# Sums of W_out on GpSimd instead of from memory, and a new place for one strip's input loads

## The chip, the cores and the metric

The kernel runs on one core of one Trainium2 chip. The core has a matrix engine (TensorE, PE in the profile), a vector engine (VectorE, DVE), an activation engine (ScalarE, ACT), a general engine (GpSimd, POOL) and a queue processor (SyncE, SP) that issues transfers between the chip's memory (HBM) and the on-chip buffer (SBUF). Matrix products land in a small accumulator memory (PSUM). The metric is the device time of one execution in microseconds, as the median of several runs.

## What is computed

An attention block without softmax, and then a feed-forward block, all in 32-bit floats (the weights of the second block arrive as 64-bit floats and are converted on the chip):

```
kv  = einsum('bhsd,bhse->bhde', k, v)          # 8 batches, 8 heads, 576 tokens, 64 features
att = einsum('bhsd,bhde->bhse', q, kv)
att = att / sqrt(mean(att**2, -1) + 1e-6) * g_norm
x   = att as (8*576, 8*64)                      # 4608 tokens x 512
h   = x @ w_in                                  # 512 -> 2048
out = maximum(h, 0)**2 @ w_out                  # 2048 -> 512
```

## The kernel before

**Strips.** The 4608 tokens are worked on in nine strips of 512 tokens, numbered 0 to 8. Each strip has an "up" stage (x times W_in, with the squared relu) and a "down" stage (the result times W_out). Products of 2 by 2 blocks are made with seven block products instead of eight (the Strassen-Winograd scheme): some blocks are first added or subtracted, and the seven products are then added up. Strip 0 multiplies plainly going up and uses the scheme once going down. Strip 1 uses it once going up and twice, nested, going down. Strips 2 to 8 use it nested both ways, so that each of their stages consists of 7 times 7 small products, and each small product is 16 matrix instructions in the trace (lines 841 to 842).

**The weights of the down stage.** For each of the seven outer products p, W_out has a combined block (`w_out`, in HBM). The inner seven products need, beside three of its quarters (b11, b12, b22, products 1, 2 and 3 in the order of the loop), four further sums, numbered 5, 6, 7 and 4: b12 - b11, then b22 minus that, then b22 - b12, then b21 minus the second. `deep_sums` (line 1028) makes these four on VectorE, once, while strip 0 goes down; `store_deep_sums` (line 969) stores them in `w_deep` in HBM. In every strip from 1 on, `stream` (line 933) loads for each p two tiles of six buffers: three quarters of `w_out` (768 KB) and the four sums of `w_deep` (1024 KB). A buffer is loaded again when TensorE has read what it held.

**The order of the work.** It is written out by hand: the order in which the program emits instructions is the order on each engine. A strip from 2 on has 55 "slots" of the up stage (`up_slot`, line 1248) and then 14 steps of the down stage (`down_deep`, line 1109, two steps for each of the outer products in the order 4, 1, 2, 6, 5, 7, 3). Products 1, 2 and 4 of the first outer product (p = 4) already stand in slots 49, 51 and 53; its products 7, 5, 6 and 3 come in the second step of the down stage:

```
        if k == 0 and s >= DEEP_UP:
            if i == 0:
                return
            for j in (7, 5, 6, 3):
                small_products(s, p, (j,))
```

For the other p, the first step makes products 1, 2, 3, the second 4, 5, 6, 7. VectorE makes the sums on the activations' side (`leaf_steps`, tiles `g_s`, lines 1046 and 289), and adds up the products (`together`, tiles `o_sb`, line 1088). GpSimd works in the up stage: sums of x for the next products (`leaf_x`, `sum_x`, line 289, tiles `x_l` and `x_t`), additions to intermediate results (line 1300, tiles `snap` and `gt`), and at the end of the up stage four additions of activations that the nested down stage needs (`add_s1`, line 1184, `gt<-gt`), one earlier and three in slots 47 to 50. In the down stage it has nothing to do until the last outer product, where it begins the sums of x for the next strip.

**The loads.** All of them are issued on SyncE's queue, in the order of the program; a load waits there for its buffer, and what stands behind it waits too. Loads of keys and values (256 KB each), of the remaining rows of a batch, and of queries (64 KB pieces, in order, called drips) are not emitted where they are used. The main loop (from line 1338, the choice of loads from line 1405) runs a clock of its own, estimated in microseconds per slot, and emits a load when it is due, except where `quiet` holds it back, and not closer together than `least`.

Of the kernel before, what the change touches and what calls it, by code (L numbers as in the profile page):

```python
# [20 lines left out]
def kernel(  # L21
# [198 lines left out]

    w_out = dram.tile([7, P, 2, FQ, P], FP32, name="w_out")

    w_deep = dram.tile([7, P, 4, FQ // 2, P], FP32, name="w_deep")

    w_in_deep = dram.tile([7, P, 3, 2, WN // 2], FP32, name="w_in_deep")

# [706 lines left out]
    def stream(n=1):  # L933
        for _, u in zip(range(n), to_stream):
            p = u[2] if u[0] == "in" else u[1]
            t = stream_pool.tile([P, 4, FQ // 2, P], FP32, name="w_blk", tag="w_blk")
            if u[0] == "in":
                w_blk[u] = t.rearrange("p n f e -> p n (f e)")
                nc.sync.dma_start(out=w_blk[u][:, 0:3], in_=w_in_deep[A_IN[p]].rearrange("p n g e -> p n (g e)"))
            elif len(u) == 2:  # L940
                w_blk[u] = t.rearrange("p (h a) f e -> p h (a f) e", h=2)
                nc.sync.dma_start(out=w_blk[u], in_=w_out[B_OUT[p]])
            elif u[2] == 0:

                nc.sync.dma_start(
                    out=t[:, 1:4], in_=w_out[B_OUT[p]].rearrange("p h (a f) e -> p (h a) f e", a=2)[:, 1:4]
                )
                for i, j in enumerate((3, 1, 2)):
                    w_blk[*u[:2], j] = t[:, i + 1]
            else:  # L950
                nc.sync.dma_start(out=t, in_=w_deep[B_OUT[p]])
                for i, j in enumerate((5, 6, 7, 4)):
                    w_blk[*u[:2], j] = t[:, i]

    def out_tile():
# [13 lines left out]
    def store_deep_sums(p, w):  # L969
        if p in (6, 4):  # L970

            parts = [sum_pool.tile([P, FQ // 2, P], FP32, name=f"w_t{i}", tag="sum") for i in range(4)]
            for _ in deep_sums(parts, w):
                if p == 4:
                    yield
            for i, t in enumerate(parts):
                nc.sync.dma_start(out=w_deep[B_OUT[p], :, i], in_=t)
            return
        if p not in deep:
            reserve(p)  # L980
        t = deep.pop(p)
        deque(deep_sums([t[:, i] for i in range(4)], w), 0)
        nc.sync.dma_start(out=w_deep[B_OUT[p]], in_=t)

    def down(s, p, i):
        if i == 0:
# [71 lines left out]
    LAST_PLACE = {1: (0, 0), 2: (1, 0), 6: (1, 1), 5: (2, 0), 7: (2, 1), 4: (3, 0), 3: (4, 0)}  # L1058
    place = lambda s, p: LAST_PLACE if s == N_STRIP - 1 and p in (5, 3) else PLACE

    def small_products(s, p, js):
        c = "B" if p in (4, 2, 5, 3) else "A"
        if js[0] == 1 and p not in (6, 7, 3):
            opened[c] = set()
            n = 2 + (s == N_STRIP - 1 and p == 5)
            chain[c] = [fpsum.tile([P, 4, P], FP32, name=f"ps_{c}", tag="f") for _ in range(n)]
            if n == 3:
                chain[c].append(apsum.tile([P, 2, 4, P], FP32, name="ps_x", tag="x", bufs=1)[:, 0])
                chain[c].append(apsum.tile([P, 4, P], FP32, name="ps_at", tag="at"))
        for j in js:  # L1070
            x, i = place(s, p)[j]
            a, w = leaf[p][j], w_blk.pop((s, p, j))
            for f in range(FQ // 2):
                halved_product(
                    chain[c][x][:, i, :], a[:, f, :], w[:, f, :], x not in opened[c] and f == 0, f == FQ // 2 - 1
                )
            opened[c].add(x)
# [31 lines left out]
    def down_deep(s, k, i):  # L1109
        p = DEEP_ORDER[k]  # L1110
        if k == i == 0:
            stream()
        if s == N_STRIP - 1 and k == 6 and i == 1:

            o = out_tile()
            q, rest = (t.rearrange("p t (h e) -> p (t h) e", h=2) for t in (o, part[6]))
            at = {j: chain["B"][x][:, i : i + 1] for j, (x, i) in place(s, p).items()}
            sums = {
                1: [(slice(0, 4), 1)], 6: [(slice(1, 2), 2), (slice(2, 4), 6), (slice(0, 1), 6)],
                7: [(slice(2, 3), 5), (slice(2, 3), 7), (slice(0, 1), 5), (slice(3, 4), 7)],  # L1120
                4: [(slice(3, 4), 4)], 3: [(slice(0, 1), 3)],
            }
            for js in ((1,), (2, 6), (5, 7), (4,), (3,)):
                small_products(s, p, js)
                for to, j in sums[js[-1]]:
                    n = to.stop - to.start
                    nc.vector.tensor_tensor(
                        out=q[:, to], in0=rest if j == 1 else q[:, to], in1=at[j].to_broadcast([P, n, P]), op=ALU.add
                    )
                    if (j, to.start) in ((2, 1), (7, 2), (4, 3), (3, 0)):  # L1130
                        eng = nc.scalar if j == 3 else nc.sync
                        send_quarter(s, 0, 1, o, *divmod(to.start, 2), eng)
# [6 lines that stand above are left out]
            stream(2)  # L1139
            deque(leaf_next[1], 0)  # L1140
            for slot in sorted(relus):
                relu_squares(slot)
            for slot in sorted(first_s):
                add_s1(s, slot)
            return
        if k == 6 and i == 1:
            small_products(s, p, (4,))
            return
        if s < N_STRIP - 1 or k < 6:
            small_products(s, p, ((1, 2, 3), (4, 5, 6, 7))[i])  # L1150
        if k < 6:
            stream()
        q11, q12, q21, q22 = (gq[s, q] for q in (11, 12, 21, 22))
        if i == 1:
            if k == 0:
                nc.vector.tensor_tensor(out=q12, in0=q12, in1=q22, op=ALU.add)
            if k == 3:
                minus(nc.vector, q22, q22, q11)
            if k == 4:
                minus(nc.vector, q21, q21, q11)  # L1160
            if k == 6:
                deque(together(s, p), 0)
            return
        if k == 2:
            minus(nc.vector, q11, q12, q11)
        if k == 3:
            leaf_sums(s, DEEP_ORDER[k + 1])
        if k:
            deque(together(s, DEEP_ORDER[k - 1]), 0)
        if k < 6 and k != 3:  # L1170
            leaf_sums(s, DEEP_ORDER[k + 1])
        if k == 6 and s + 1 < N_STRIP:
            leaf_x(s + 1, 0)
            sum_x(s + 1, 5)
            sum_x(s + 1, 6)
            leaf_x(s + 1, 1)
# [71 lines left out]
    def up_slot(s, slot):  # L1248

        for n, p in enumerate(UP_SETS):  # L1250
            i, odd = divmod(slot - 7 * n, 2)
            if not odd and 0 <= i < 7:
                up_small(s, n, p, ORDER[i], slot)
        if slot in SUM_AT:
            sum_x(s, SUM_AT[slot])
        n, at = divmod(slot, 7)
        if at == 0 and 0 < n < 6:
            leaf_x(s, n + 1)
        if s == DEEP_UP and at == 0 and n < 7:
            deep_differences_in(A_IN[UP_SETS[n]])  # L1260
        relu_squares(slot)
        add_s1(s, slot)
        if slot in (1, 3, 5):
            small_products(s - 1, 3, ((slot + 9) // 2,))
        if slot == 5:
            stream()
            deque(together(s - 1, 3), 0)
        if slot == 40:
            leaf_next.update({4: leaf_steps(s, 4), 1: leaf_steps(s, 1)})
        if slot in (49, 51, 53):  # L1270
            small_products(s, 4, ({49: 1, 51: 2, 53: 4}[slot],))
        if slot in (41, 43, 45, 47):
            next(leaf_next[4])
        if slot in (49, 51):
            next(leaf_next[1])
# [62 lines left out]
    for s in range(N_STRIP):  # L1338
# [25 lines left out]
        for i, (w, fn, a) in enumerate(steps):  # L1364
# [33 lines left out]
            if s:  # L1398
                clock[0] += 3.2 if i >= n_up else 2.2 if s == DEEP else 1.2
                soon = tiles_due and tiles_due[0][2][0] // NT == s + 1  # L1400
                if i == n_up + 10:
                    while tiles_due and tiles_due[0][2][0] // NT == s + 1:
                        _, f, a = tiles_due.popleft()
                        f(*a)
                elif not due(keys_due) and not (soon and due(tiles_due)):
                    least = 2.1 if s == DEEP else 4.5 if i < n_up else 3.3
                    quiet = n_up * 2 // 3 < i < n_up + 3 or s == DEEP and i > n_up + 9
                    quiet = quiet or s == DEEP and i < n_up and drips and drips[0][0] == load_q_rest
                    if not quiet and clock[0] >= dripped[0] + least:
                        dripped[0] = clock[0]  # L1410
                        drip(True)
# [73 lines left out]
```

## Time and profile before

| | us |
|---|---|
| median of three runs | 879.48 |
| the three runs | 876.89, 879.48, 882.86 |
| the profiled execution | 876.18 |
| its span in the profile | 874.4 |
| TensorE busy | 860.8 |
| VectorE busy | 722.9 |
| ScalarE busy | 352.0 |
| GpSimd busy | 315.4 |
| median from issue to landing, `w_deep` tile of 1024 KB | 7.2 |
| the same, `w_out` tile of 768 KB | 6.7 |

The span is the time from the first to the last recorded instruction; the execution takes 1.8 us more. TensorE's matrix instructions are pipelined and overlap in the record, so "busy" does not mean that it is at its peak, but an idle stretch of TensorE is a real gap. A digit in the lines of tenths stands for a fortieth of the span (21.9 us), and 9 is 90% or more. The 56 loads of `w_deep` and the 56 of `w_out` are eight strips times seven outer products.

### The profile page before, as it was taken

The numbers are of one execution on the slowest core, as the hardware profiler recorded it, in microseconds if no ns is written. First come the engines' busy times: TensorE is split into PE (matmuls) and PEld (weight loads), VectorE is DVE, ScalarE is ACT, GpSimd is POOL, SyncE is SP. The second block draws the span as 40 slices with busy tenths as digits, with TensorE's granted clock in tenths as the row PEclk, the third lists the DMA queues.
The fourth block names the chain that finished last, engine by engine and source line by source line (L and its number), as shares of the span: only waits on it lengthen the run. The fifth ranks groups of instructions, "written<-read, shape, count | busy, mean of one in ns | idle before, by whom it ended". The sixth has DMA issues, their size and how long they took to land.

```text
span 874.4 us, 32665 instructions
## 1 busy us (share of the span) xinstructions
PE 860.8 (98%) x14176; PEld 805.8 (92%) x14176; DVE 722.9 (83%) x1236; ACT 352.0 (40%) x805; POOL 315.4 (36%) x319
## 2 busy tenths in 40 slices
PE   8999999999999899999999999999999999999998
PEld 7445888889999899999999999999999999999998
DVE  3899998879867896889778977897889777975897
ACT  5799241320047402560358034811392147202710
POOL 1100004630458305650475045704471447144700
PEclk9999999999999999999999999999999999999999
DMA  9998998999988997989778978998668856885483
GB/s 306 328 311 251 285 372 237 283 339 346 305 219 205 338 328 242 239 290 338 245 213 261 344 268 228 271 346 287 189 238 293 295 173 218 299 283 196 175 313 120
DMA packets 170304, 236.49 MB, mean 270 GB/s; under 512 B 79536, under 2 KB 134576, under 8 KB 161840
## 3 DMA queue, kind: packets, MB, share of 16 engines
q1 hardware_dynamic: 169856, 234.33, 82.5%
q8 instruction: 111, 1.82, 0.8%
q14 instruction: 33, 0.27, 0.1%
q10 hardware_dynamic: 304, 0.07, 0.0%
HBM read 197.66 MB, written 36.70 MB: 268 GB/s over the span
## 4 chain that ended last, share of the span: by engine, by line
PE 82%; DVE 9%; DMA 4%; ACT 3%; issue 2%; SPq 1%; DVEq 0%; ACTq 0%
PE ps_A L842 35%; PE ps_B L842 30%; PE ps_C L842 5%; PE ps_A L847 4%; PE x_ps L468 2%; PE kv_ps L432 2%; PE ps_B L847 2%; DVE w_c L269 1%; DVE w_t L289 1%; DMA q<-in_q_dram 1%; DMA w_blk<-w_deep 1%; DMA w_deep<-w_t 1%; DVE wt L289 1%; DMA q_rest<-in_q_dram 1%; PE ps_C L847 1%
## 5 line engine op out<-in xcount | busy, mean ns | idle before, releaser
L842 PE MATMUL ps_B<-w_blk,g_s 128*64 128x128 f32 x2016 | 122.6, 273 | 0.0
L842 PEld LDWEIGHTS ps_B<-w_blk,g_s 128*64 128x64 f32 x2016 | 113.1, 137 | 0.1
L842 PE MATMUL ps_A<-x_l,w_in 128*64 128x128 f32 x1568 | 102.4, 273 | 0.6 <-ACT snap L1305 0.6
L289 POOL TENSOR_TENSOR x_l<-xT 128x256 f32<-128x256 f32 x21 | 15.9, 757 | 232.4 <-PE ps_A L842 184.3
L842 PE MATMUL ps_B<-w_blk,gt 128*64 128x128 f32 x1504 | 94.7, 273 | 2.8 <-DMA w_blk<-w_deep 1.6
L842 PE MATMUL ps_A<-w_blk,g_s 128*64 128x128 f32 x1536 | 92.7, 273 | 0.4 <-issue 0.4
L842 PEld LDWEIGHTS ps_A<-x_l,w_in 128*64 128x64 f32 x1568 | 88.9, 137 | 0.9 <-ACT snap L1305 0.8
L842 PEld LDWEIGHTS ps_B<-w_blk,gt 128*64 128x64 f32 x1504 | 85.1, 137 | 3.6 <-issue 2.2
L1300 POOL TENSOR_TENSOR snap<-snap,gt 128x512 f32<-128x512 f32 x35 | 46.2, 1319 | 113.1 <-ACT snap L1305 107.5
L842 PEld LDWEIGHTS ps_A<-w_blk,g_s 128*64 128x64 f32 x1536 | 86.1, 137 | 0.5 <-issue 0.5
L1305 ACT COPY snap<-ps_A 128x512 f32<-128x512 f32 x63 | 36.8, 585 | 105.0 <-PE ps_A L842 99.0
L1240 ACT ACTIVATE gt<-gt 128x512 f32<-128x512 f32 x112 | 70.1, 626 | 14.2 <-DVE gt L1300 14.2
L1241 ACT ACTIVATE gt<-gt 128x512 f32<-128x512 f32 x112 | 70.7, 631 | 3.6
L842 PE MATMUL ps_A<-w_blk,gt 128*64 128x128 f32 x1152 | 71.5, 273 | 0.0
L842 PEld LDWEIGHTS ps_A<-w_blk,gt 128*64 128x64 f32 x1152 | 65.0, 137 | 0.0
L1089 ACT COPY o_sb<-ps_A 128x128 f32<-128x128 f32 x24 | 6.4, 265 | 145.5 <-PE ps_A L842 110.2
L1088 DVE TENSOR_TENSOR o_sb<-o_sb,ps_B 128x256 f32<-128x256 f32 (+1 forms) x123 | 47.4, 386 | 15.8 <-ACT o_sb L1089 11.0
L289 DVE TENSOR_TENSOR gt<-gt 128x2048 f32<-128x2048 f32 (+1 forms) x29 | 59.7, 2063 | 0.0
L1300 POOL TENSOR_TENSOR gt<-gt,snap 128x512 f32<-128x512 f32 x42 | 52.6, 1282 | 17.7 <-DVE snap L1300 17.7
L842 PE MATMUL ps_B<-x_l,w_blk 128*64 128x128 f32 x784 | 51.3, 273 | 0.0
L842 PE MATMUL ps_A<-x_l,w_blk 128*64 128x128 f32 x784 | 51.2, 273 | 0.0
L1046 DVE TENSOR_TENSOR g_s<-gt 128x512 f32<-128x512 f32 x56 | 47.9, 856 | 0.0
(194 smaller groups left out, 1801.6 us busy)
## 6 DMA issues: line engine op xcount, KB each, us to landing
w_blk<-w_deep SPq DMA_DIRECT2D x56, 1024.0 KB, 7.2
w_blk<-w_out SPq DMA_DIRECT2D x56, 768.0 KB, 6.7
w_blk<-w_in_deep SPq DMA_DIRECT2D x49, 768.0 KB, 6.1
raw<-in_moe_w_in_dram SPq DMA_DIRECT2D x16, 512.0 KB, 7.0
raw<-in_moe_w_out_dram SPq DMA_DIRECT2D x16, 512.0 KB, 4.8
k<-in_k_dram SPq DMA_DIRECT2D x29, 256.0 KB, 4.8
v<-in_v_dram SPq DMA_DIRECT2D x29, 256.0 KB, 5.1
x_d<-x_q SPq DMA_DIRECT2D x27, 256.0 KB, 5.3
```

The costliest lines, as they stand in the source:

```text
L269: yield nc.vector.scalar_tensor_tensor(out=ci, in0=high, scalar=-(2**30), in1=ci, op0=ALU.bitwise_and, op1=ALU.bitwise_or)
L289: eng.tensor_tensor(out=out, in0=a, in1=b, op=ALU.subtract)
L432: nc.tensor.matmul(ps[ts(h, D), i], lhsT=a, rhs=w, start=i == 0 and c == 0, stop=c == C, skip_group_check=True)
L468: nc.tensor.matmul(ps[half, r, i, ts(p, D)], lhsT=q[row, half], rhs=kvd[b, p][row, row], start=True, stop=True)
L842: nc.tensor.matmul(ps[half], lhsT=lhsT[:, half], rhs=rhs, start=start, stop=stop, skip_group_check=True)
L847: nc.tensor.matmul(bank[BANK[p]][:, i, :], lhsT=lhsT(k), rhs=rhs(k), start=p in (1, 5, 2) and i == 0 and k == 0, stop=k == n - 1, skip_gro ...
L1046: nc.vector.tensor_tensor(out=t, in0=a21, in1=a22, op=ALU.add)
L1088: add = lambda out, a, b: nc.vector.tensor_tensor(out=out, in0=a, in1=b, op=ALU.add)
L1240: nc.scalar.activation(o, o, AF.Relu)
L1241: nc.scalar.activation(o, o, AF.Square)
L1300: add = lambda eng, out, a, b: eng.tensor_tensor(out=out, in0=a, in1=b, op=ALU.add)
L1305: nc.scalar.copy(t, ps)
```

## The change

Two things are changed.

The second of the four further sums (number 6) is no longer stored in `w_deep` nor loaded. It is still made on VectorE in strip 0, because the fourth is made from it, but `w_deep` has three parts, and a load of it moves 768 KB into the last three quarters of its buffer. The free first quarter is filled by a new function `second_sum`, which subtracts on GpSimd: quarter b22 of the `w_out` tile minus the first sum. It is emitted for the next outer product in the second step of each but the last, so that it stands one outer product ahead of its use; for p = 4 it is emitted in slot 50 of the up stage (in strip 1, at the first step of the down stage).

The second thing concerns the main loop in strip 2 (`DEEP_UP`). In its slots 25 to 38 keys, values and remaining rows are not emitted when due, and from slot 24 on no queries are; in the first 15 slots of strip 3 queries may follow each other every 2.1 instead of 4.5 us of the loop's clock. In the order of SyncE's queue, two pairs of keys and values, and one pair of remaining rows, move from ahead of strip 2's first two W_out tiles to behind them, and four pairs of query pieces move from strip 2 to the beginning of strip 3. The order on TensorE, VectorE and ScalarE is the same as before; GpSimd's has the 56 new subtractions, seven in a row in each strip from 1 on, with nothing between them.

```diff
-    w_deep = dram.tile([7, P, 4, FQ // 2, P], FP32, name="w_deep")
+    w_deep = dram.tile([7, P, 3, FQ // 2, P], FP32, name="w_deep")
...
-                nc.sync.dma_start(out=t, in_=w_deep[B_OUT[p]])
-                for i, j in enumerate((5, 6, 7, 4)):
+                nc.sync.dma_start(out=t[:, 1:4], in_=w_deep[B_OUT[p]])
+                for i, j in enumerate((6, 5, 7, 4)):
                     w_blk[*u[:2], j] = t[:, i]
...
-            for i, t in enumerate(parts):
+            for i, t in enumerate((parts[0], *parts[2:])):
                 nc.sync.dma_start(out=w_deep[B_OUT[p], :, i], in_=t)
...
-        deque(deep_sums([t[:, i] for i in range(4)], w), 0)
-        nc.sync.dma_start(out=w_deep[B_OUT[p]], in_=t)
+        deque(deep_sums([t[:, i] for i in (1, 0, 2, 3)], w), 0)
+        nc.sync.dma_start(out=w_deep[B_OUT[p]], in_=t[:, 1:4])
...
+    def second_sum(s, p):
+
+        if s >= DEEP:
+            minus(nc.gpsimd, w_blk[s, p, 6], w_blk[s, p, 3], w_blk[s, p, 5])
...
         if k == i == 0:
             stream()
+            if s == DEEP:
+                second_sum(s, p)
+        if i == 1 and k < 6:
+            second_sum(s, DEEP_ORDER[k + 1])
...
+        if slot == 50:
+            second_sum(s, 4)
...
-                elif not due(keys_due) and not (soon and due(tiles_due)):
-                    least = 2.1 if s == DEEP else 4.5 if i < n_up else 3.3
-                    quiet = n_up * 2 // 3 < i < n_up + 3 or s == DEEP and i > n_up + 9
+                elif not (not (s == DEEP_UP and 24 < i < 39) and due(keys_due)) and not (soon and due(tiles_due)):
+                    least = 2.1 if s == DEEP or s == DEEP_UP + 1 and i < 15 else 4.5 if i < n_up else 3.3
+                    quiet = n_up * 2 // 3 < i < n_up + 3 or s == DEEP and i > n_up + 9 or s == DEEP_UP and i > 23
```

## The prediction

> **What bounds the kernel now.** I first read the page: the span, the engines' totals and GpSimd's tenths.
>
> ```profile
> span 874.4 us, 32665 instructions
> PE 860.8 (98%) x14176; PEld 805.8 (92%) x14176; DVE 722.9 (83%) x1236; ACT 352.0 (40%) x805; POOL 315.4 (36%) x319
> ...
> POOL 1100004630458305650475045704471447144700
> ```
>
> TensorE sets the time. All its idle time is 874.4 - 860.8 = 13.6 us, and 4.4 us of that lies in the first 120 us and 2.6 in the last 46, which the change does not touch. So there is little to gain, and any new gap of TensorE is paid in full. GpSimd has one slice at 0 or 1 in nearly every strip, in the down stage. Next, what TensorE waits for, in the list of waits:
>
> ```profile
> PE ps_B L842 <- DMA w_blk<-w_deep: 1.6, 1, 1.6
> ...
> PE ps_B L842 <- DMA w_blk<-w_out: 1.2, 1, 1.2
> ```
>
> In eight strips TensorE waits only twice for a W_out tile. The timeline of TensorE shows both at strip 2's first outer product (slots 49 to 53):
>
> ```profile
> 288.29 1.09 PE L842 MATMUL ps_B<-w_blk,gt 128*64 128x128 f32 x16 [1.17 <-DMA w_blk<-w_out]
> ...
> 290.93 1.07 PE L842 MATMUL ps_B<-x_t,w_blk 128*64 128x128 f32 x16
> 293.64 1.09 PE L842 MATMUL ps_B<-w_blk,gt 128*64 128x128 f32 x16 [1.64 <-DMA w_blk<-w_deep]
> 294.54 1.07 PE L842 MATMUL ps_A<-x_l,w_in 128*64 128x128 f32 x16
> ```
>
> Then I looked at the same place in an undisturbed strip, on GpSimd, TensorE and VectorE (strip 3; the three views in this order):
>
> ```profile
> 380.50 1.67 POOL L1300 TENSOR_TENSOR snap<-snap,gt 128x512 f32<-128x512 f32 x1 [3.62 <-ACT snap L1305]
> 382.13 5.11 POOL L1184 TENSOR_TENSOR gt<-gt 128x512 f32<-128x512 f32 x3
> ```
> ```profile
> 386.29 3.66 PE L842 MATMUL ps_B<-w_blk,g_s 128*64 128x128 f32 x64
> ```
> ```profile
> 384.93 1.17 DVE L289 TENSOR_TENSOR g_s<-g_s,gt 128x512 f32<-128x512 f32 x1
> 386.02 0.68 DVE L1300 TENSOR_TENSOR gt<-ps_B,snap 128x512 f32<-128x512 f32 x1
> ...
> 387.22 0.68 DVE L289 TENSOR_TENSOR g_s<-gt,g_s 128x512 f32<-128x512 f32 x1
> 387.82 0.68 DVE L289 TENSOR_TENSOR g_s<-gt 128x512 f32<-128x512 f32 x1
> ```
>
> The 64 matrix instructions from 386.29 are p = 4's products 7, 5, 6 and 3. GpSimd is still in its three additions until 387.24. Where these overlap a VectorE operation that reads two SBUF tiles (`g_s`), that one takes 1.17 instead of 0.68 us and an addition about 1.72 instead of 1.28; a VectorE operation that reads PSUM stays at 0.68.
>
> **Loads: 256 KB less, 56 times.** 14.7 of 236.5 MB go. From rows of the page, a 768 KB tile lands after 6.7 us and a 1024 KB tile after 7.2, so each lands some 0.5 us sooner. Apart from the two waits above, none of these tiles is late, so this is worth **0**. The stores in strip 0 shrink too; there TensorE's only related gap is 0.3 us, which I leave as a bound.
>
> **Strip 2's loads moved: a gain.** Ahead of the `w_deep` tile issued at 284.87 (it took 8.63 us to land) SyncE's queue held 1 MB of keys and values, 0.25 MB of remaining rows and six query pieces. Its buffer had been read by about 278.4. With those behind it, it should land before 287, and the `w_out` tile, whose buffer was free from 272.3, well before that. Both waits, 1.17 + 1.64 = 2.81 us, go. What is late next is VectorE: the product of 290.93 reads a bank that VectorE finishes at 290.42, in a stretch in which it is busy without a gap (287 to 293.8). Moved up by 1.17 it would start at 289.76, so it waits about 0.6 us. Gain: **2.2 us**, between 0.4 (the second wait stays, and the first is worth 1.17 less VectorE's 0.6, rounded down) and 2.8. The moved keys are used at 336 and have over 40 us to spare. The moved query pieces are different: two sets that VectorE transposes at 353.1 and 354.3 are now issued in strip 3's first slots, partly behind stores that left at 343.6, so the last should land near 351 or 352 by the 3 to 6 us of the rows there. I take 0 for it, with 3 us (half a load's latency) as the far end.
>
> **56 subtractions on GpSimd.** Each is 128x512 with both inputs in SBUF: 1.28 us undisturbed, 1.72 beside VectorE, so 72 to 96 us in all, on an engine with 30 us idle in each down stage. For 49 of them that hides everything: the subtraction of p runs when its `w_deep` tile has landed, on most strips 2.4 to 6 us before product 4 of p reads that tile, and product 6 comes two products (1.75 us) later still. In strip 1 the first tile lands at 196.4 and product 6 starts near 200.7. The seventh subtraction of a strip delays the sums of x for the next strip, which stand behind it in GpSimd's queue: in strip 3 from 417.12 to about 420.4 (the last `w_deep` tile lands at 418.68), in strip 1 from 229.8 to 236. TensorE reads these sums 7.6 to 10.8 us after they are ready, so that costs 0 too.
>
> The other seven are those of p = 4 in strips 2 to 8. They stand in GpSimd's queue behind the three additions, and TensorE needs them at the third of the 64-instruction block's four products, 2 x 0.873 = 1.75 us after its start. After the additions the subtraction takes 1.70 more (beside the two `g_s` of 387.22 and 387.82, at the spacing of the additions before it), and TensorE starts 0.13 later (293.64 after a landing at 293.51).
>
> | strip | additions end | sum ready, TensorE starts (+1.83) | product 6 now | new gap |
> |---|---|---|---|---|
> | 3 | 387.24 | 389.07 | 388.04 | 1.03 |
> | 4 | 476.06 | 477.89 | 477.26 | 0.63 |
> | 5 | 569.76 | 571.59 | 570.36 | 1.23 |
> | 6 | 658.44 | 660.27 | 659.58 | 0.69 |
> | 7 | 746.40 | 748.23 | 747.19 | 1.04 |
> | 8 | 831.97 | 833.80 | 832.77 | 1.03 |
>
> That is **5.65 us**. In strip 2 the additions end at 292.63, so TensorE could start at 294.46, and product 6 (now 297.16) moves to 294.9: no gap. If VectorE does not disturb it, 0.47 less each: 2.8. If each is held up by both `g_s`, 0.45 more: 8.4. Behind the waiting product TensorE's whole queue waits, and later stages have no slack that gives it back.
>
> [...]
>
> **Contention in the down stages.** In the window from 392 to 424 us VectorE is busy 29.8 of 32 us, so it has 0.42 us to spare per outer product (6.11 us). A subtraction takes about 0.47 from it, at worst 1.1 (the longest disturbed `g_s` took 1.8). The sum that TensorE waits for first is ready 2.5 to 4.3 us ahead, so lagging by 0.05 per product costs 0; by 0.7, with seven of them, the lead is gone.
>
> **Sum.** On the profiled execution: 876.2 - 2.2 + 5.65 = 879.6. The median of the runs shown lies 3.3 above that execution, and the result will be a median as well, so 879.5 + 3.45 = **882.9**, rounded to 883.
>
> **Rivals.**
> - *The sum is in time* (the additions finish sooner, or TensorE's queue of weights hides it): only strip 2's gain is left, 879.5 - 2.2 = 877.3, faster than before. For it: 1.72 is needed each time, and an undisturbed subtraction leaves gaps of 0.2 to 0.8 only. Against: in all six strips the additions end 0.8 to 1.2 us before the product. Chance 0.18.
> - *VectorE becomes the bound in the down stages*: decided by 0.42 us to spare against what a subtraction really takes. At 1.1 each, 7 x 0.7 = 4.9 of lag less 2.5 of lead, 2.4 us a strip, eight strips: 19, and with the forecast's 3.45 some 902; at half that, 892. Together with late queries in strip 3: chance 0.12.
> - *The waits in strip 2 don't go* (the tile is held by its buffer or by the stores before it): 879.5 + 5.65 - 0.4 = 884.7. Chance 0.08.
> - The forecast: 0.62.
>
> **Range and chances.** About 1% (8.8 us) is what a measurement of this kernel can tell from no change. From the first rival's 877 to the forecast with the far ends of the sum and the queries, 879.5 - 2.2 + 8.4 + 3 = 888.7, taken at 888. Faster by over 1% would need most of TensorE's 13.6 us: 0.02. Slower by over 1% is the second rival: 0.12. The rest is 0.86.
>
> **What would show it.** Right: TensorE's waits name GpSimd's subtraction (`w_blk`, line 289) six or seven times, near 1 us each, always at the block of 64; the two waits for W_out tiles are gone; `g_s` operations in the down stages are longer on average than now (0.69), and no TensorE wait names them. Wrong: no such wait, waits for `g_s` or `o_sb` in the down stages, or a wait of VectorE's transposes for `q` near 351. The largest risk is a subtraction whose waits for four transfers cost GpSimd more than I can see here.

## The result, and the profile after

The changed kernel takes 881.8 us (median of 22 executions, 876.3 to 887.4) beside 877.2 us for the kernel before (22 executions, 873.5 to 882.9): a ratio of **1.0039 (1.0022 to 1.0057)**, or +3.4 us (1.9 to 5.0); the two medians differ by 4.6 us, which lies inside this interval. The prediction said +3.45, and 882.9 as the time. The total is right, but it came about in another way than was worked out, as the traces show. In the table of the experiments below, one execution of the kernel that holds strip 3's queries and keys too (1122 us at a mean clock of 0.75) is left out.

The page of the changed kernel: span, engine totals, and the tenths of GpSimd.

```profile
span 880.0 us, 32793 instructions
PE 862.8 (98%) x14176; PEld 806.2 (92%) x14176; DVE 755.9 (86%) x1236; ACT 352.5 (40%) x805; POOL 402.6 (46%) x375
...
POOL 1100004622468544743577255735474547455731
```

GpSimd has 56 instructions and 87 us more, and its empty slices in the down stages have filled. VectorE has the same 1236 instructions and 33 us more, which is 0.59 us for each subtraction; without the subtractions it falls back to 723.3 us (an experiment below). TensorE's busy time is 2.0 us longer with the same 14176 instructions, a first sign that some of them ran slower.

What TensorE waits for, in the list of waits (us in total, times, longest):

```profile
PE ps_B L842 <- DMA w_blk<-w_deep: 4.0, 1, 4.0
...
PE ps_B L842 <- DVE g_s L289: 1.7, 1, 1.7
...
PE ps_B L842 <- POOL w_blk L289: 1.2, 3, 0.5
PE ps_B L842 <- DVE snap L1311: 1.1, 1, 1.1
```

Strip 2's two waits are gone, and VectorE's wait of 1.1 us stands in their place. But there are three new ones. The timeline of TensorE shows the largest, in **strip 3**, and the queue of SyncE when the tile was issued (the kernel before, then the changed one):

```profile
381.05 1.04 PE L842 MATMUL ps_B<-w_blk,gt 128*64 128x128 f32 x16
...
378.04 0.38 SPq L951 DMA_DIRECT2D w_blk<-w_deep  x1
```
```profile
378.08 1.04 PE L842 MATMUL ps_B<-w_blk,gt 128*64 128x128 f32 x16
...
380.70 1.04 PE L842 MATMUL ps_B<-x_t,w_blk 128*64 128x128 f32 x16
385.77 1.09 PE L842 MATMUL ps_B<-w_blk,gt 128*64 128x128 f32 x16 [4.03 <-DMA w_blk<-w_deep]
386.67 1.57 PE L842 MATMUL ps_A<-x_l,w_in 128*64 128x128 f32 x16
387.96 4.94 PE L842 MATMUL ps_B<-w_blk,g_s 128*64 128x128 f32 x64
...
381.25 0.38 SPq L951 DMA_DIRECT2D w_blk<-w_deep  x1
```

This is the first `w_deep` tile of strip 3. TensorE came to the first outer product there 2.97 us earlier than before (378.08 and 381.05), but the tile was issued 3.21 us later (381.25, before 378.04) and landed at 385.64. The wait costs more than 4.03 us. The 16 instructions of 386.67 took 1.29 us to the next start, where others take 0.88, and the block of 64 took 4.74 where it takes 3.49. In the table by windows of 2 us (busy time of PE, PEld, DVE, ACT, POOL, then the granted clock, the DMA share and GB/s) the reason is in the column after POOL:

```profile
384.00:386.00 2.00, 0.23 (x4) 0.26 (x6) 0.00 (x0) 1.03 (x2) 0.50 (x2) 1.00 1.00 384
386.00:388.00 2.00, 2.00 (x33) 2.00 (x31) 0.00 (x0) 0.00 (x0) 1.03 (x1) 0.78 0.99 381
388.00:390.00 2.00, 2.00 (x23) 2.00 (x21) 1.73 (x3) 0.97 (x2) 0.05 (x1) 0.50 1.01 418
390.00:392.00 2.00, 2.00 (x36) 2.00 (x34) 0.17 (x1) 0.29 (x1) 1.30 (x1) 0.87 0.38 153
392.00:394.00 2.00, 2.00 (x41) 2.00 (x39) 1.41 (x4) 0.27 (x1) 0.00 (x0) 1.00 0.42 83
```

After the stall the granted clock fell to 0.50. The record of the clock in the trace has it there from 387.10 to 390.51, which agrees with the means of these windows. That is another 0.41 + 1.25 = 1.7 us, and the stall is worth 5.7 in all.

In **strips 4 to 8** TensorE does wait for GpSimd's sum of p = 4, as forecast, but less. Strip 5, on GpSimd, VectorE and TensorE:

```profile
567.79 5.11 POOL L1193 TENSOR_TENSOR gt<-gt 128x512 f32<-128x512 f32 x3
572.87 1.27 POOL L289 TENSOR_TENSOR w_blk<-w_blk 128x512 f32<-128x512 f32 x1
```
```profile
572.88 1.80 DVE L289 TENSOR_TENSOR g_s<-gt,g_s 128x512 f32<-128x512 f32 x1
574.61 1.76 DVE L289 TENSOR_TENSOR g_s<-gt 128x512 f32<-128x512 f32 x1
```
```profile
571.77 1.92 PE L842 MATMUL ps_B<-w_blk,g_s 128*64 128x128 f32 x32
574.19 1.97 PE L842 MATMUL ps_B<-w_blk,g_s 128*64 128x128 f32 x32 [0.51 <-POOL w_blk L289]
```

The subtraction starts as soon as the additions end and takes 1.27 us, as undisturbed ones in this profile do (1.28 at 407.17); it is VectorE's `g_s`, issued 0.01 us later, that takes 1.80 instead of 0.68. By starts of TensorE's instructions the five gaps cost 0.19, 0.72, 0.18, 0.56 and 0.55: 2.2 us.

In **strip 1** TensorE waits for VectorE, whose two `g_s` take 1.69 and 1.10 us instead of 0.68 beside GpSimd's work (GpSimd, VectorE, TensorE):

```profile
233.09 1.28 POOL L289 TENSOR_TENSOR w_blk<-w_blk 128x512 f32<-128x512 f32 x1 [5.49 <-DMA w_blk<-w_deep]
```
```profile
233.23 1.69 DVE L1046 TENSOR_TENSOR g_s<-gt 128x512 f32<-128x512 f32 x1
234.96 1.10 DVE L289 TENSOR_TENSOR g_s<-g_s,gt 128x512 f32<-128x512 f32 x1
```
```profile
236.97 1.09 PE L842 MATMUL ps_B<-w_blk,g_s 128*64 128x128 f32 x16 [1.71 <-DVE g_s L289]
```

So the account of the profiled execution is: strip 1 +1.7; from there to the beginning of strip 3 -4.7 (2.97 ahead, in spite of the 1.7); strip 3 +5.7; strips 4 to 8 +2.2; in all +4.9 of the 5.6 by which the spans differ. Of the other 0.7, 0.6 is a break of TensorE at 704.21 for which the trace names no other engine.

### The profile page after: what moved, and what is told of

The parts are those of the page before. It is cut to its first block, busy times and chain, and to the rows that moved or that the text cites. A ratio compares the mean times of both kernels' runs of the same rounds, so it can differ in the third digit from the quotient of the medians.

```text
span 880.0 us, 32793 instructions
## 1 busy us (share of the span) xinstructions
PE 862.8 (98%) x14176; PEld 806.2 (92%) x14176; DVE 755.9 (86%) x1236; ACT 352.5 (40%) x805; POOL 402.6 (46%) x375
## 4 chain that ended last, share of the span: by engine, by line
PE 79%; DVE 9%; ACT 3%; DMA 3%; POOL 2%; issue 2%; SPq 1%; DVEq 0%; POOLq 0%; ACTq 0%
PE ps_A L842 30%; PE ps_B L842 25%; PE ps_A L847 6%; PE ps_C L842 4%; PE ps_B L847 3%; DVE g_s L289 2%; PE kv_ps L432 2%; PE x_ps L468 2%; PE ps_C L847 2%; DVE o_sb L1093 1%; PE ps_A L888 1%; POOL gt L1193 1%; DVE g_s L1046 1%; ACT gt L1250 1%; PE ps_B L888 1%
## 5 line engine op out<-in xcount | busy, mean ns | idle before, releaser
L289 POOL TENSOR_TENSOR w_blk<-w_blk 128x512 f32<-128x512 f32 x56 | 83.7, 1498 | 197.1 <-DMA w_blk<-w_deep 157.3
L842 PE MATMUL ps_B<-w_blk,g_s 128*64 128x128 f32 x2016 | 124.8, 275 | 3.2 <-DVE g_s L289 1.7
L289 DVE TENSOR_TENSOR g_s<-gt 128x512 f32<-128x512 f32 x56 | 58.6, 1047 | 0.0
L1046 DVE TENSOR_TENSOR g_s<-gt 128x512 f32<-128x512 f32 x56 | 54.3, 969 | 0.0
L289 DVE TENSOR_TENSOR g_s<-gt,g_s 128x512 f32<-128x512 f32 x56 | 51.0, 910 | 2.0
```

The costliest lines, as they stand in the source:

```text
L289: eng.tensor_tensor(out=out, in0=a, in1=b, op=ALU.subtract)
L842: nc.tensor.matmul(ps[half], lhsT=lhsT[:, half], rhs=rhs, start=start, stop=stop, skip_group_check=True)
L1046: nc.vector.tensor_tensor(out=t, in0=a21, in1=a22, op=ALU.add)
```

## The experiments

Each kernel was timed beside the kernel before on the same chip. All ratios are to that kernel, with 95% intervals; us are at 878. Rows 2 to 5 were timed in one set, rows 6 to 8 in a second and the last three in a third, each with its own executions of the kernel before (35, 23 and 29), so a difference of two rows carries both intervals.

| kernel | ratio | us |
|---|---|---|
| the changed kernel | 1.0039 (1.0022 to 1.0057) | +3.4 |
| sums alone | 1.0039 (1.0010 to 1.0068) | +3.4 |
| load order alone | 1.0001 (0.9972 to 1.0030) | +0.1 |
| sum of p = 4 ahead of two additions | 1.0002 (0.9977 to 1.0027) | +0.2 |
| query pieces let go in the down stage | 0.9987 (0.9962 to 1.0011) | -1.1 |
| no subtractions | 0.9971 (0.9950 to 0.9991) | -2.5 |
| the two edits together | 0.9983 (0.9959 to 1.0007) | -1.5 |
| strip 3's queries and keys held too | 1.0086 (1.0054 to 1.0118) | +7.6 |
| the good order, no sums | 0.9957 (0.9927 to 0.9986) | -3.8 |
| both edits, strip 3's keys held | 0.9971 (0.9948 to 0.9994) | -2.5 |
| the good order, strip 3's keys held, no sums | 0.9956 (0.9939 to 0.9974) | -3.9 |

### The two parts, each alone

Sums alone: the changed kernel with the main loop's lines of before.

```diff
-                elif not (not (s == DEEP_UP and 24 < i < 39) and due(keys_due)) and not (soon and due(tiles_due)):
+                elif not due(keys_due) and not (soon and due(tiles_due)):
...
-                    quiet = n_up * 2 // 3 < i < n_up + 3 or s == DEEP and i > n_up + 9 or s == DEEP_UP and i > 23
+                    quiet = n_up * 2 // 3 < i < n_up + 3 or s == DEEP and i > n_up + 9
```

> The part with the sums alone: second_sum on GpSimd and three parts in w_deep, the main loop as it was before the change. My prediction on record gives this part +5.65 us over the kernel before, as six TensorE waits of 0.6 to 1.2 us for GpSimd's sum at the block of 64, and none in strip 1. The theory from the trace of the changed kernel gives about +4: a wait of about 1.7 us for g_s at the end of strip 1, gaps of at most 0.7 us (some 2.7 in all) at the blocks of 64 in strips 3 to 8, and strip 2's two waits for W_out tiles (2.8 us before) still there, each up to 0.5 shorter because the tiles are smaller. If the sums cost nothing but contention off the path, +0.

Measured: +3.4 us (0.9 to 6.0). GpSimd's gaps are those of the changed kernel. The waits for `g_s` add up to only 0.5 us there, in three pieces, two of them in strip 1 (0.4), so the 1.7 us is not in every execution. Strip 2 waits for its W_out tiles (0.57 and 0.78 us). Not expected by either theory: the first `w_deep` tile of strip 3 was late here too, by 3.2 us, with the old order.

```profile
PE ps_B L842 <- DMA w_blk<-w_deep: 3.7, 2, 3.2
...
PE ps_B L842 <- POOL w_blk L289: 1.2, 3, 0.5
```

Order alone: the kernel before with the changed loop, `w_deep` with four parts, no `second_sum`.

> The part with the load order alone: the main loop of the changed kernel, w_deep with four stored sums and nothing new on GpSimd. My prediction on record gives -2.2 us against the kernel before. Theory of the give-back: strip 2 gains 4.7 (the two W_out waits and the 1.3 us gap near 264 go, VectorE's 1.1 comes), but the first w_deep tile of strip 3 lands late because the held-back query pieces crowd SyncE's queue at the start of strip 3: a TensorE wait of 4 to 6 us there, and a granted clock near 0.5 to 0.9 for about 4 us after it, 1.9 us more, so +1 to +3 in all. Rival, that the late tile comes of VectorE being held up by the new subtractions: no wait in strip 3 here, and -4 us or more.

Measured: +0.1 us (-2.5 to +2.6), which by itself does not tell -2.2 from +1 to +3. The trace does: strip 2 has no wait for a W_out tile any more, and strip 3 has one of 6.08 us, with no subtraction anywhere in the kernel. The gain is there and is given back. VectorE held up by subtractions cannot be what makes this tile late here. The profiled execution (884.8 us) is the slowest of the twelve, so 6.08 is not the usual size of the wait.

```profile
380.35 1.04 PE L842 MATMUL ps_B<-x_t,w_blk 128*64 128x128 f32 x16
387.47 1.98 PE L842 MATMUL ps_B<-w_blk,gt 128*64 128x128 f32 x16 [6.08 <-DMA w_blk<-w_deep]
389.20 1.95 PE L842 MATMUL ps_A<-x_l,w_in 128*64 128x128 f32 x16
```

### The sum of p = 4 ahead of two additions

```diff
+        if slot == 47:
+            second_sum(s, 4)
         add_s1(s, slot)
...
-        if slot == 50:
-            second_sum(s, 4)
```

> The whole change, but the sum of p = 4 is emitted in slot 47 ahead of the last two of GpSimd's three additions (before: behind all three). Theory that the additions ahead of it in GpSimd's queue make it late: the five gaps at the blocks of 64 in strips 4 to 8 (2.2 us in the changed kernel) go and no TensorE wait names GpSimd's w_blk; the wait of 4.0 us in strip 3 and the one in strip 1 stay. About -2.2 us against the changed kernel, +1.2 against the one before. Rival, that it is the contention for SBUF between the sum and VectorE wherever it stands: the gaps stay or turn into waits for g_s, 0 us.

Measured: 1.0002 against 1.0039 for the changed kernel, 3.2 us less (the two intervals overlap by a little). No TensorE wait names GpSimd's sum any more, and the block of 64 in strip 4 runs without a gap. The sum now stands between the additions:

```profile
474.66 1.73 POOL L1193 TENSOR_TENSOR gt<-gt 128x512 f32<-128x512 f32 x1
476.35 1.73 POOL L289 TENSOR_TENSOR w_blk<-w_blk 128x512 f32<-128x512 f32 x1
478.04 2.98 POOL L1193 TENSOR_TENSOR gt<-gt 128x512 f32<-128x512 f32 x2
```

It takes 1.73 here, longer than the 1.27 behind the additions, and still costs nothing, since it is ready at 478.1 and used at 481. The cost in strips 4 to 8 came of the place in GpSimd's queue; the longer time beside VectorE, which is still there, does not bring it alone. The wait in strip 3 stayed (2.8 us).

### The query pieces let go in strip 2's down stage

```diff
-                    quiet = ... or s == DEEP_UP and i > 23
+                    quiet = ... or s == DEEP_UP and 23 < i < n_up
```

> The whole change, but the query pieces are held back only to the end of strip 2's up stage and follow in its down stage (the changed kernel holds them to the end of strip 2). Theory of the crowded queue: the first w_deep tile of strip 3 is issued 3 us or more earlier, TensorE's wait of 4.0 us for it goes or shrinks below 1, the granted clock stays 1.00 there, and strip 2's gain is kept: about -5.9 us against the changed kernel, some 875 to 876 us, -2 to -2.5 against the kernel before. Rival, VectorE held up by the subtractions, or the throttled queue of the transposed rows (xT) alone: the wait stays above 3 us and the time within 1 us of the changed kernel's.

Measured: 0.9987 against 1.0039, 4.6 us less. The tile was issued at 375.92 (381.25 in the changed kernel) and landed 0.22 us before its use; no TensorE wait names a W_out tile, and the granted clock there is 1.00 throughout. What is left are the waits for the sums:

```profile
PE ps_B L842 <- DVE g_s L289: 2.1, 2, 1.3
PE ps_B L842 <- POOL w_blk L289: 1.8, 5, 0.5
```

The holding back of the queries is where strip 2's gain went. SyncE's queue ahead of the tile shows how close it is. First the changed kernel, then this one:

```profile
363.68 0.57 SPq L939 DMA_DIRECT2D w_blk<-w_in_deep  x1
364.29 4.23 SPq L123 DMA_DIRECT2D q<-in_q_dram  x4
368.62 2.78 SPq L654 DMA_DIRECT2D x_d<-x_q  x1
...
378.39 2.76 SPq L661 DMA_DIRECT2D xT<-x_d  x4
381.25 0.38 SPq L951 DMA_DIRECT2D w_blk<-w_deep  x1
```
```profile
361.21 0.57 SPq L939 DMA_DIRECT2D w_blk<-w_in_deep  x1
361.82 2.45 SPq L123 DMA_DIRECT2D q<-in_q_dram  x4
364.37 2.34 SPq L654 DMA_DIRECT2D x_d<-x_q  x1
...
374.06 1.76 SPq L661 DMA_DIRECT2D xT<-x_d  x4
375.92 0.38 SPq L951 DMA_DIRECT2D w_blk<-w_deep  x1
```

The same 19 transfers stand between the two tiles in both. They took SyncE 17.6 us there and 14.7 here, and they began 2.5 us later there. From the end of strip 2 (near 333) to this tile SyncE issued 24 query pieces in the changed kernel, remaining rows counted, 16 here, and 12 in the kernel before.

### Each kernel once more

The kernel before, unchanged:

> The kernel before, unchanged, profiled once more. In the runs beside the last experiments 25 of 35 executions of it had a mean granted clock below 1 (0.996 to 0.998), where the profiled one had 1.000; a stall of TensorE of some 3 us or more was followed by a low clock in the changed kernel. Theory that the first w_deep tile of strip 3 is late by chance in the kernel before too: a TensorE wait of 2 to 5 us for a W_out tile in strip 2 or 3 with a clock below 1 after it, a time of 878 to 883. Rival, that the 4.0 us wait belongs to the change: no wait above 2 us, clock 1.000, about 875 to 877.

The stall of the changed kernel meant there is the one of 4.03 us, the only one above 3 us in its profile. Measured: 882.5 us, clock 0.996, and a wait of 5.27 us in strip 2, for the `w_out` tile, where the first profile has 1.17. Strip 3's first `w_deep` tile was late by 0.4 us. The long wait:

```profile
286.51 1.04 PE L842 MATMUL ps_B<-x_l,w_blk 128*64 128x128 f32 x16
292.82 1.98 PE L842 MATMUL ps_B<-w_blk,gt 128*64 128x128 f32 x16 [5.27 <-DMA w_blk<-w_out]
```

So a wait above 2 us for a W_out tile does not belong to the change alone. The profile of before that the prediction stands on is one of its better executions: of 87 executions beside these experiments 31 had a mean clock of 1.000, as that one had. The changed kernel:

> The changed kernel, profiled once more. Three kernels with its load order waited 1.8, 2.8 and 6.1 us for the first w_deep tile of strip 3, as it did itself (4.0). Theory that the order puts this tile late in nearly every execution: a wait of 1.5 to 6 us there again, none for a W_out tile in strip 2, a wait of 1 us or more for g_s at the end of strip 1, and GpSimd gaps of 0.2 to 0.5 us at the blocks of 64. Rival, that the 4.0 us were chance: no wait there, and a time near 877.

Measured: 878.7 us, and the wait in strip 3 again, though the clock stayed at 1.000 after it; GpSimd's four waits add up to 1.5 us, and the wait at the end of strip 1 was 0.4 us instead of 1.7.

```profile
384.66 1.09 PE L842 MATMUL ps_B<-w_blk,gt 128*64 128x128 f32 x16 [3.11 <-DMA w_blk<-w_deep]
```

### No subtractions

```diff
-            minus(nc.gpsimd, w_blk[s, p, 6], w_blk[s, p, 3], w_blk[s, p, 5])
+            w_blk[s, p, 6] = w_blk[s, p, 5]
```

> The whole change without the 56 subtractions: product 6 reads the first sum in place of the second, so the second sum is left out of the result. What the subtractions cost: theory, 1.7 us in strip 1 and 2.2 in strips 4 to 8, no wait for GpSimd's w_blk or g_s is left, VectorE is busy some 723 us again; but TensorE comes to the first w_deep tile of strip 3 up to 1.7 us sooner and waits for it as much longer, so -2.2 to -3.9 us against the changed kernel (0 to +1.5 against the one before). Rival, that the late tile of strip 3 comes of the subtractions (VectorE held up): that wait goes too, and the time is 6 us or more below the changed kernel's.

Measured: 0.9971 against 1.0039, 6.0 us less. That is more than the 2.2 to 3.9 expected and as much as the rival's, but not in the rival's way, which was that the wait in strip 3 goes: it stayed (1.8 us). VectorE's busy time fell back to 723.3 us and no wait names `g_s` or GpSimd's sum. The other 2 to 4 us would be there if the subtractions also lengthen strip 3's wait; one profile does not show that, and this one is the fastest of the twelve.

### Both edits, and what more can be held back

> The last two together: sum of p = 4 in slot 47, and the query pieces let go in strip 2's down stage. If the two costs are separate, they add up: -3.3 and -3.4 us against the changed kernel, about 875 us, -3 to -4.5 against the kernel before. Rival, that what is saved at the blocks of 64 is waited for again at the first w_deep tile of strip 3 (which had 0.2 us to spare in the profile of the second): about 877, as that one alone.

Measured: 0.9983, beside 1.0002 and 0.9987 for each alone; whether they add up cannot be told within these intervals. Its trace has no wait for a W_out tile or a GpSimd sum, and 0.2 us to spare in strip 3. Then strip 3 treated as strip 2:

```diff
-                    quiet = ... or s == DEEP_UP and 23 < i < n_up
+                    quiet = ... or s in (DEEP_UP, DEEP_UP + 1) and 23 < i < n_up
```

> The same, and strip 3 treated as strip 2: keys and values held in its slots 25 to 38, query pieces from slot 24 to the end of its up stage. Theory that the first w_deep tile of strip 3 is late because of what stands ahead of it in SyncE's queue: it is issued 4 us or more ahead of where it was, with 3 us or more to spare, the granted clock is 1.00 in nearly all executions, and the time is 0.5 to 1.5 us below the kernel without this step, with a smaller spread. Rival, that the pieces pushed on crowd strip 4 in the same way: a wait there for a w_deep tile or for the queries, and the time the same or 2 to 5 us more.

Measured: +7.6 us. The tile of strip 3 now has 3.9 us to spare, and the rival is right: the queries held back in strip 3 are late in strip 4. VectorE waits to transpose them, and TensorE 8.8 us behind it.

```profile
450.81 0.71 DVE L384 STREAM_TRANSPOSE qT<-q 128x512 f32<-128x512 f32 x1 [10.69 <-DMA q<-in_q_dram]
```

With only the keys, values and remaining rows held in strip 3:

```diff
-                elif not (not (s == DEEP_UP and 24 < i < 39) and due(keys_due)) and ...
+                elif not (not ((s == DEEP_UP and i > 24 or s == DEEP_UP + 1 and i > 14) and i < 39) and due(keys_due)) and ...
```

> Sum of p = 4 in slot 47, query pieces let go in strip 2's down stage, and in strip 3 the keys, values and remaining rows (1.25 MB) held in slots 15 to 38, so that they stand behind its first w_deep tile in SyncE's queue. Theory that this tile is late because of what stands ahead of it: it is issued 3 us or more earlier and has 3 us or more to spare (0.2 without this), the granted clock is 1.00 in nearly all executions; the time is 0 to 1 us below the kernel without this step (875.3) and the spread smaller. Rival, that the held keys are late in their turn: a TensorE wait for k, v or the products made from them in strip 3's down stage or strip 4, and 1 us or more on top.

Measured: 0.9971 (0.9948 to 0.9994). The tile has 2.4 us to spare, but the transfers held back now stand ahead of the `w_out` tile of the next outer product, and TensorE waits 1.4 us for that one. Whether it gains over the kernel without this step (0.9983) cannot be told within the intervals; the spread is no smaller, and 7 of 12 executions have a mean clock of 1.000.

### The order without the sums

> No sum on GpSimd (w_deep with four stored sums, as before the change); of the load order the part that held: keys and query pieces held behind strip 2's first W_out tiles, the query pieces let go again in its down stage. Tells whether the sums are worth anything beside it. Theory that the sums only cost (contention with VectorE, 256 KB less per load worth nothing): the time is equal to or up to 2 us below that of the kernel with both (875.3), -3 to -5 us against the kernel before. Rival, that the smaller tiles matter at the first w_deep tile of strip 3 (1024 KB land some 0.5 us later than 768): TensorE waits there for up to 1 us more, the clock is below 1 in more executions, and the time is 0.5 to 2 us above 875.3.

Measured: **0.9957 (0.9927 to 0.9986)**, 3.8 us below the kernel before, and not above the same order with the sums (0.9987 and 0.9983). In its profile strip 3's tile was late by 2.4 us all the same, after 20.4 us of SyncE's time for the same 19 transfers, so the order reduces these waits and does not end them.

> The load order of the last kernel without any sum on GpSimd (four stored sums). If both theories hold, this is the fastest: 872.5 to 874.5, -3.5 to -5.5 us against the kernel before, no TensorE wait for a W_out tile in strips 2 and 3, none for g_s or GpSimd's w_blk. Rival, that loading 14.7 MB more keeps SyncE's queue at its limit: waits of 0.5 us or more for W_out tiles remain, and the time is that of the kernel with the sums, or above.

Measured: **0.9956 (0.9939 to 0.9974)**, 3.9 us below the kernel before, with a mean clock of 1.000 in 11 of 12 executions. 1.2 us are left to spare for strip 3's first tile; the next `w_out` tile is waited for:

```profile
PE ps_A L842 <- DMA w_blk<-w_out: 1.2, 1, 1.2
```

This kernel and the last have the lowest ratios, and neither has a sum on GpSimd. They are not alone below the kernel before: the interval of the kernel with both edits and strip 3's keys held, which has the sums, also ends below 1 (0.9994), and the three intervals overlap.

## Why the prediction was right, and where it was wrong

- **The total** (+3.45; measured +3.4): right by luck, as the sum of two errors that cancel. The forecast made the sums cost 5.65 and the order gain 2.2. Alone they measured +3.4 (0.9 to 6.0) and +0.1 (-2.5 to +2.6). Both forecasts lie inside these intervals, so it is the traces and the further experiments, not these two times, that show the errors.
- **The sums of p = 4 behind the additions**: the mechanism is right, and the experiment with the sum moved ahead removes exactly these waits. The term that was mis-sized is the 1.70 us for a subtraction beside two `g_s`: in strips 4 to 8 it measured 1.26 to 1.29, where the subtraction is issued first and VectorE's `g_s` is the one that takes longer. With it come 2.2 us in strips 4 to 8, where the forecast has 4.6; the bound "if VectorE does not disturb it" was the value to take. In strip 3 nothing was left of the gap, since TensorE came to the block after the longer wait for the tile. The sign that the forecast named, six or seven waits near 1 us, was not met: the trace names three, of 0.3 to 0.5.
- **Who is slowed**: the prediction took 1.72 us for a GpSimd operation beside a `g_s`, from rows of the kernel before. In the changed kernel's profile, where the subtraction began first, by 0.01 us in strip 5 and 0.14 in strip 1, it took 1.27 and 1.28, and the `g_s` 1.80 and 1.69. Where the two engines alternate, in the three additions of strip 5 (5.11 us together), both are slower: 1.70 instead of 1.28, and 1.17 instead of 0.68.
- **Contention in the down stages costs 0**: wrong by 0.3 to 2.4 us, the sum of TensorE's waits for `g_s` in the profiles with sums. A subtraction takes 0.59 us of VectorE's time, not 0.47. In strips 4 to 8 no such wait is seen, but TensorE waited in strip 1, and in some executions at the end of strip 2 or 3. The sign that the forecast named, "no TensorE wait names them", was not met.
- **Strip 2's loads: a gain of 2.2**: right that both waits go and VectorE's bank is late next (1.1 us, forecast 0.6). By starts of TensorE's instructions the two waits are worth 1.39 + 1.79 and VectorE's costs 1.25, so 1.9 in all. The 4.7 us of the account above are more because gaps that name no engine (`issue`, 1.34, 0.39 and 0.41 us in the profile of before) were absent; other profiles of both orders have some of them.
- **The moved query pieces cost 0**: this is the step that failed. It looked at the transposes that use them, and those were indeed in time. It did not follow what stands behind them in SyncE's queue for the next 30 us, up to the first `w_deep` tile of strip 3, although it named that tile's counterpart in strip 2 as late for this very reason. Nor did it count all that moves: beside four pairs of query pieces, four pairs of remaining query rows left strip 2's down stage, and three of them came ahead of that tile in strip 3. Letting the queries go earlier gave back 4.6 us. The order does not decide alone: the tile was late by 1.8 to 6.1 us in all five profiles with the changed order, by 0, 0.4 and 3.2 us in the three with the old one, and by 0, 0 and 2.4 us in the three with the query pieces let go and nothing held in strip 3.
- **256 KB less per load is worth 0**: not settled. The forecast had each tile land 0.5 us sooner. The medians from issue to landing are 5.5 to 5.8 us for `w_deep` with the smaller load (5.6 in the changed kernel) and 6.8 to 7.5 with the larger (7.2 in the kernel before), and those of `w_out`, whose size is the same, fell too (5.4 to 5.8 beside 6.2 to 6.7; 5.4 and 6.7 in these two). Once strip 3's tile is late, that is time for TensorE. The kernel without subtractions (0.9971) and the order alone (1.0001) have the same order and no sum on GpSimd and differ in these loads: 2.6 us less with the smaller ones, but the intervals overlap. The kernels of the good order without sums change the loads and the sums at once and do not tell the two apart.
- **The profile as a base**: the forecast took the one profiled execution as typical and moved it by 3.3 us to the median of three. Over 22 executions the median was 877.2, only 1.0 above that execution, and 879.0, 878.0 and 879.3 in the later sets. Stalls for W_out tiles and the low clock after them, as in the second profile of before (5.27 us, then a mean clock of 0.78 from 294 to 300), are a likely reason; which executions have them is not shown beyond that profile. The spread of the three times before, 876.9 to 882.9, was the hint: they differ by more than any wait of TensorE in that profile.

Still open is how long SyncE needs for the 19 transfers ahead of strip 3's tile in a given execution: 14.7 to 20.4 us over the profiles in which the order of these 19 is the same (16.1 in the first profile of before, 19.7 for the sums alone), and nothing tried here fixes it.

## What to carry to other kernels

A transfer that is moved back in a queue can be paid for by an urgent transfer behind it, even when its own user is in time (here a tile issued 3.21 us later, and a wait of 4.03 us): walk down the queue from its new place to the next tile with little time to spare, and compare issue times there. When work is put on an idle engine, look at what is ahead of it in that engine's queue at its tightest use, and put it ahead if its inputs are there (here the ratio fell from 1.0039 to 1.0002). If the mean clock of the profiled execution is higher than that of most others, its waits may be among the fewest there are, not the usual ones (here a longest wait for a W_out tile of 1.64 us at a clock of 1.000, and of 5.27 in a second profile at 0.996).

## What the runs showed of the hardware that was not expected

- **A stall of TensorE was paid twice.** After 4.03 us the granted clock fell to 0.50 and cost 1.7 us more; around waits of 5.27, 6.08 and 8.8 us it fell as well (lowest means over 6 us: 0.66, 0.57 and 0.52). It also fell in four executions after 1.8 to 2.4 us (lowest means over 6 us: 0.72 to 0.77; in three of them just before the small products of the attention block), and did not after 2.4, 2.8, 3.11 and 3.2 (1.00 there). The spell at 0.50 lasted 3.41 us in the changed kernel's profile; by the means over 6 us, taken at 0.50, the spells come to about 3.4 us in four more profiles, 6.8 in two and 10.2 in one. So a mean clock of 0.998 over 877 us would be one spell of 3.41 us and 0.996 two, an estimate from these lengths. The length of a wait alone does not tell the two groups apart here: the clock fell after 1.8 us and not after 3.2.
- **SyncE had at most eight transfers in flight** in the first profile of before and in that of the changed kernel (by issue and landing times). With eight in flight, 118 times in the one and 94 in the other, the next was issued 0.016 us after a landing at the soonest. Among the transfers ahead of strip 3's tile in the changed kernel, single 64 KB query pieces held SyncE's queue for 0.32 to 1.66 us.
- **A `g_s` of VectorE took 1.80 us instead of 0.68 beside a GpSimd subtraction of 128x512** that was issued 0.01 us ahead of it and took 1.27 (strip 5 of the changed kernel). Both read two SBUF tiles.
